# Attention, then a squared-relu layer pair, on one core: second part of P.V in a layer bank, x transposed by pairs, planner constants anew

## The chip, the core and the metric

The kernel runs on one core of one Trainium2 chip. A core has five engines that run side by side: TensorE (PE, matmul), VectorE (DVE), ScalarE (ACT), GpSimd (POOL) and SyncE (SP). DMA queues move data between HBM and SBUF. Matmuls write to PSUM, which has eight banks. The metric is the time of one execution in microseconds (us).

## The reference

The inputs are q, k and v of 8 batches x 8 heads x 576 tokens x 64 columns, a bias table of 32 buckets x 8 heads, and two weights, 512 x 2048 and 2048 x 512. All are float32.

```python
scores = (1.0 / np.sqrt(D)) * np.matmul(q, k.transpose(0, 1, 3, 2))
scores = scores + bias_table[bucket].transpose(2, 0, 1)[None]   # bucket of |i - j|, one value from 128 on
attn = softmax(scores)                                          # over the last axis
x = np.matmul(attn, v).transpose(0, 2, 1, 3).reshape(4608, 512)
h = np.maximum(x @ moe_w_in, 0.0)
return h * h @ moe_w_out
```

## The kernel before

**Work in pairs and groups.** Attention works on 32 pairs of heads, four to a batch; `pair(p)` (line 580) plans one. The two layers work on 9 groups of 512 tokens of x; `layers(g)` (line 1026) plans layer 1 of group g and layer 2 of group g - 1. A batch has 576 tokens, so group 0 needs batch 0, and group 1 needs the last 64 tokens of batch 0 and the first 448 of batch 1.

**A pair.** For the first three batches q and k are loaded with a cast to float16 in rows of six tokens and turned on PE: twelve transposes of 96 x 64 for q and as many for k (line 608), two heads side by side in two halves of the output partitions. DVE or ACT copies each to `qt` or `kt` (lines 570, 572). From batch 3 on (DT_QK) a DMA turns them. Score matmuls (line 653) have 64 rows, one head in each half of the array; they fill one of two sets of two PSUM banks (`st`). The last 64 queries and the last 64 keys of both heads get matmuls of their own (677, 702) from small zero-padded copies `qz` (635). ACT takes the exponentials (664, 687, 712). DVE multiplies the band near the diagonal by a table of exp(bias) (745, four bands a pair). That table is made at the start by 96 small matmuls (353) and six copies (367).

**P.V.** The product with v (781, 788) is made in five tiles of 128 queries, of which three form part 1 and two part 2. Both parts write the one bank `pv`. A column of constants in v gives the softmax sum. DVE takes the reciprocal (805) and multiplies (810), which gives x in float16.

**x.** For the first three batches (DT_X) `x_turn` (838) transposes x on PE once all four pairs of a batch are done: for each of five tiles of tokens four transposes, one for each pair, into one bank (848), and one copy of 512 columns (256 for the last tile) to `xt`. From batch 3 on a DMA turns x pair by pair (826).

**The layers.** Layer 1 of a group has 16 pieces of four matmuls of 512 columns (1044). Each piece goes to a relu (1065 on ACT, 1067 on DVE) and a square on DVE (1075). Layer 2 is a Strassen-Winograd product: seven products, each in two halves of eight matmuls of 256 columns (962), in the order P_ORDER, with sums of activations (921) and of weights (901) on DVE. Products 1 and 2 share a bank, 5 and 3 share one, and 7 and 4 share one; the second of each two waits until the first is read (989, 995, 997).

**What sets the order.** The program is not written in its final order. Each step is given to a planner (`Plan`, line 94) with an estimated cost for each engine that may run it, its inputs, the buffers it needs, a due time and an earliest time. `Plan.schedule` takes, again and again, the step that can start first, by due time among equals, and so fixes the order on every engine and, where two engines may run a step, which of them does. An engine runs its list strictly in order. PERIOD, LEAD, FAST and FASTN give the due time of a pair (`nominal`, 559), AHEAD how far ahead of it a pair may start, G0 and GP the due times of the groups, QUIET and LATER the earliest times of fills, TAB that of the bias table, and EV the pair up to which q/k copies are kept on DVE (pairs 1 to EV - 1; pair 0 is free). A change of any constant can move every step.

**PSUM.** Three banks (`f`, ring `r_g`) serve everything but scores and P.V: q/k transposes, the bias table, x transposes, layer 1 and layer 2.

**Loads.** POOL issues the loads of q, k, v and the weights in a fixed order. ORDER gives the place of the four quarters of w_in (i) and w_out (o) among batch 1's second two pairs (q1, k1), pairs 4 and 5 (q0, k0) and v. POOL also makes some of the `qz` copies, in the same queue. q and k of pair 0 come uncast by SP and ACT, and `cast_first` (463) casts them on DVE and ACT.

Of the kernel before, what the change touches and what calls it, by code (L numbers as in the profile page):

```python
# [25 lines left out]
GT = 512  # L26
NG = B * S // GT
XB = 3
XR = XB * S
DT_QK = 3  # L30
PERIOD, LEAD, FAST, FASTN = 9600.0, 1600.0, 3000, 7
AHEAD, G0, GP = 20600.0, 54700.0, 35900.0
DT_X = 3
RELU_DVE = 2
NSTG, NQK, NPT, NV, NX, NGB, NRT, NY = 5, 4, 3, 3, 6, 2, 4, 4
QUIET, LATER = 5200.0, 8500.0
TAB, EV = 6400.0, 1
P_ORDER = "1 6 2 5 7 3 4"
P_LAST = "1 6 2 5 7 3 4"
SIX = 3  # L40
ORDER = "k0 i0 q0 q1 v i1 i2 o0 k1 o1 i3 o2 o3"
HALF = GT // 2


# [146 lines left out]
def kernel(  # L191
# [71 lines left out]

    def loader(eng_name, eng, out_, in_, packets, deps=(), bufs=(), due=0.0):

        lane = [Buf(r_lane)] if eng_name == "POOL" else []
        issue = P.add(
            {eng_name: 720.0 if eng_name == "POOL" else 600.0},  # L270
            lambda: io(eng.dma_start(out=out_(), in_=in_())),  # L271
            deps,
            list(bufs) + lane,
            due,
        )
        return P.add({"DMA": packets / 16}, None, [issue], list(bufs) + lane, due if lane else -1e9), issue
# [6 lines left out]
    def const(f):  # L283
        return lambda: f

    def load(eng_name, eng, out_, in_, packets, deps=(), bufs=(), due=0.0):
        return loader(eng_name, eng, out_, in_, packets, deps, bufs, due)[0]


    first_f = gs[NGB - 1].bitcast(FP32).rearrange("p t c -> p (t c)")  # L290
# [9 lines left out]
    l_bt = load(  # L300
        "ACT", nc.scalar, const(bt_sb),
        const(bass.AP(tensor=bias_table.tensor, offset=bias_table.offset, ap=[[0, 4]] + [list(x) for x in bias_table.ap])),
        128 * 27, due=0,
    )
    l_far = load("ACT", nc.scalar, const(far_sb), const(bias_table[NBK - 1 : NBK, :]), 27, due=1)
    l_oh = load("SP", nc.sync, const(oh_sb), const(oh_d.ap()), 128 * 60, due=4)
# [15 lines left out]
    z_one = P.add({"DVE": 60.0}, lambda: io(nc.vector.memset(one_sb, 1.0)), due=-2)  # L322
    far_b = Buf(r_g)
    o_far = P.add(
        {"PE": 250.0},
        lambda: io(nc.tensor.matmul(g_ps[far_b.slot][:, 0:8], one_sb, far_sb, start=True, stop=True)),
        [l_far, z_one], [far_b], 0.0, 0.0, "f",
    )
# [18 lines left out]
    for c in range(6):  # L347
        t_b = Buf(r_g)

        def t_mm(c=c, t_b=t_b):  # L350
            for j in range(16 * c, 16 * c + 16):
                io(
                    nc.tensor.matmul(
                        g_ps[t_b.slot][:, ts(j - 16 * c, 32)], oh_sb[:, 380 - 4 * j : 508 - 4 * j],
                        eb_sb.rearrange("p i h -> p (i h)"), start=True, stop=True,
                    )
                )

        o = P.add({"PE": 16 * 55.0}, t_mm, [o_eb, l_oh], [t_b], LEAD + TAB, 0.0, "f")

        def t_ev(o, c=c, t_b=t_b):
            src = g_ps[t_b.slot].rearrange("p (w h) -> p h w", h=H)
            dst = tb_sb[:, :, ts(c, 64)]
            if o.eng == "ACT":
                io(nc.scalar.activation(out=dst, in_=src, func=COPYF))
            else:
                io(nc.vector.tensor_copy(out=dst, in_=src))

        tabs_done.append(one_of({"DVE": dve(512), "ACT": act(512)}, t_ev, [o], [t_b], 1.0))
# [17 lines left out]
    def fill(ap, value, ns, due, after, deps=()):  # L387
        return P.add({"DVE": ns}, lambda: io(nc.vector.memset(ap, value)), deps, (), due, after)  # L388

    zz = z_sb.bitcast(FP32)  # L390
    z_fix = [[fill(zz[:, 0], 0.0, 150.0, 10, QUIET)], [fill(zz[:, 1:], 0.0, 300.0, 11, LATER)]]
    first = [
        fill(pt_sb[:, :, PW:], 1.0, 150.0, 20, LATER),
        fill(pm_sb[:, :, S:], 1.0, 150.0, 20, LATER),
    ]
    v_fix = [
        [
# [5 lines left out]
        for o in [fill(vm_sb[:, a].bitcast(FP32), 0.0, ns, 30, at)]  # L403
    ]
    s_fix = [
        fill(stg[i][w][96:128, 512:640].bitcast(FP32), 0.0, 90.0, 40 + i, 25000.0)
        for i in range(NSTG)
        for w in range(2)
    ]
# [53 lines left out]
    def cast_first(w):  # L463

        def cast(o):
            src, dst = first_f[0:96, ts(w, 768)], stg[b_stg[0].slot][w][0:96, :]
            if o.eng == "ACT":
                io(nc.scalar.activation(out=dst, in_=src, func=COPYF))
            else:
                io(nc.vector.tensor_copy(out=dst, in_=src))  # L470

        l_qk[0, w] = [one_of({"ACT": act(768), "DVE": dve(768, 2.0)}, cast, [l_first[w]], [b_stg[0]], -3.0)]
# [86 lines left out]
    def nominal(p):  # L559
        return LEAD + FAST * min(p, FASTN) + PERIOD * max(p - FASTN, 0)  # L560

    xt_ready, x_last = {}, {}
    x_bufs = {}

    def copy_to(engs_n, out_f, in_f, deps, bufs, due, fp16=True, dve_only=False):
# [14 lines left out]
    def pair(p):  # L580
# [5 lines left out]
        for w, dst in ((0, qts), (1, kts)):  # L586
# [14 lines left out]
            def tr(w=w, bank=bank):  # L601
                ps = g_ps[bank.slot].bitcast(FP16)
                t = stg[b_stg[p].slot][w]
                if b < SIX:
                    for j in range(6):
                        for e in range(2):
                            io(
                                nc.tensor.transpose(  # L608
                                    ps[ds(64 * e, 64), ts(j, 96)], six(t)[:, e, ts(j, D)],
                                    id_sb[0:96, 0:96],  # L610
                                )
                            )
                else:
                    for j in range(5):
                        io(nc.tensor.transpose(ps[:, ts(j, 128)], rows(t)[:, j, :], id_sb))

            o = P.add({"PE": 12 * 36.0 if b < SIX else 5 * mm(128)}, tr, l_qk[p, w] + [l_id], [bank, b_stg[p]], T - 3000, after, "c" if b < SIX else "f")

            def turned(bank=bank):
                ps = g_ps[bank.slot].bitcast(FP16)[:, 0:S]  # L620
# [148 lines left out]
        xb = x_bufs[p] = Buf(r_x)  # L769
        norms = []  # L770
        for part, qt0, nq in ((0, 0, 3), (1, 3, 2)):
            bank = Buf(r_pv)

            def pv(qt0=qt0, nq=nq, bank=bank):
                ps = pv_ps[bank.slot][:, 0 : nq * 130].rearrange("p (t e d) -> p t e d", t=nq, e=2)
                pt, pm = pts[pb.slot], p4s[pb.slot]
                va, vm = vas[b_v[b].slot], v4s[b_v[b].slot]
                for i in range(nq):
# [21 lines left out]
            )  # L800
            rb = Buf(r_r)

            def recip(nq=nq, bank=bank, rb=rb):
                ps = pv_ps[bank.slot][:, 0 : nq * 130].rearrange("p (t e d) -> p t e d", t=nq, e=2)
                io(nc.vector.reciprocal(out=rs[rb.slot][:, 0:nq], in_=ps[:, :, :, 64:65]))

            def norm(nq=nq, bank=bank, rb=rb, qt0=qt0):
                ps = pv_ps[bank.slot][:, 0 : nq * 130].rearrange("p (t e d) -> p t e d", t=nq, e=2)
                io(
                    nc.vector.tensor_tensor(  # L810
                        out=xs[xb.slot][:, qt0 : qt0 + nq, :].rearrange("p t (e d) -> p t e d", e=2),
                        in0=ps[:, :, :, 0:64],
                        in1=rs[rb.slot][:, 0:nq].to_broadcast([128, nq, 2, 64]),
                        op=MULT,
                    )
                )
# [18 lines left out]
                    xt_ready.setdefault(g_, []).append(t)  # L835
        return norms

    def x_turn(b, norms):
        xb = [x_bufs[4 * b + hp] for hp in range(4)]
        T = nominal(4 * b + 3)  # L840
        for qt in range(5):
            n = 128 if qt < 4 else 64
            bank = Buf(r_g)

            def tr(qt=qt, bank=bank):
                ps = g_ps[bank.slot].bitcast(FP16)
                for kk in range(4):
                    io(nc.tensor.transpose(ps[:, ts(kk, 128)], xs[xb[kk].slot][:, qt, :], id_sb))  # L848

            deps = [n_[0 if qt < 3 else 1] for n_ in norms]  # L850
            o = P.add({"PE": 4 * mm(128)}, tr, deps, [bank] + xb, T, 0.0, "f")
            t0 = (b % XB) * S + qt * 128
            for a, z in [(0, n)]:
                c = t0 + a
                e = copy_to(
                    4 * (z - a),
                    lambda a=a, z=z, c=c: xt_sb[:, :, c : c + z - a],
                    lambda a=a, z=z, bank=bank: g_ps[bank.slot].bitcast(FP16)[:, 0:512].rearrange(
                        "p (k t) -> p k t", k=4
                    )[:, :, a:z],  # L860
                    [o] + xt_free(b * S + qt * 128 + n), [bank], T,
                )
                for g_ in range((b * S + qt * 128) // GT, (b * S + qt * 128 + n - 1) // GT + 1):
                    xt_ready.setdefault(g_, []).append(e)

    f1_last = {}

# [158 lines left out]
    def layers(g):  # L1026
# [4 lines left out]
        if g < NG:  # L1031
# [3 lines left out]
            for nt in range(16):  # L1035
                bank = Buf(r_g)

                def f1(nt=nt, bank=bank):
                    c = (g * GT) % XR
                    n = min(GT, XR - c)  # L1040
                    for a, z, c in ((0, n, c), (n, GT, 0)):
                        for kk in range(4 if z > a else 0):
                            io(
                                nc.tensor.matmul(  # L1044
                                    g_ps[bank.slot][:, a:z], w_in_sb[:, kk, ts(nt, 128)],
# [8 lines left out]
        for i in range(16):  # L1054
            if i < len(atoms1):
                nt, f1, bank = atoms1[i]
                o = P.add(
                    {"PE": 4 * mm(512)}, f1, xt_ready[g] + [l_win[nt // 4]], [bank, gb1], due + i * 2000, 0.0, "f"
                )
                f1_last[g] = o  # L1060
                rb = Buf(r_rt)
# [33 lines left out]
    t_done = sums_of_weights()  # L1095
    g = 0
    for b in range(B):
        norms = [pair(4 * b + hp) for hp in range(4)]
        if b < DT_X:
            x_turn(b, norms)  # L1100
        while (g + 1) * GT <= (b + 1) * S and g < NG:
            layers(g)
            g += 1
# [35 lines left out]
```

The softmax here doesn't subtract the row's maximum and nothing guards it: scores larger than these inputs give would overflow.

## Time and profile before

| | before |
|---|---|
| median of 6 runs | 377.5 us (376.32 to 378.92) |
| the profiled execution | 377.47 us |
| its span, first to last instruction | 375.7 us |
| PE busy | 360.8 us (96%), 4046 matmuls |
| DVE / ACT / POOL busy | 269.0 / 255.2 / 178.4 us |
| mean granted PE clock | 0.999 |
| first q/k transpose on PE | 6.47 us |
| first layer 1 matmul, group 0 | 40.61 us |
| first layer 1 matmul, group 1 | 74.98 us |
| last run of layer 2 matmuls (line 962) | from 370.44 us, 1.91 us |

The profile is of one execution. A row of instructions in order of time has the start, the length, engine, line, operation, what is written from what, the count, and in brackets how long the engine had been idle and which engine ended that. The length of a matmul includes its way through the array, so the distance of two starts is the better measure of PE's time. In the table by stage each row has a stretch, its length, and for each engine the busy time and the number of instructions. In the chain of waits, a row is a stretch of the path that ended last.

### The profile page before, as it was taken

The numbers are of one execution on the slowest core, as the hardware profiler recorded it, in microseconds if no ns is written. First come the engines' busy times: TensorE is split into PE (matmuls) and PEld (weight loads), VectorE is DVE, ScalarE is ACT, GpSimd is POOL, SyncE is SP. The second block draws the span as 40 slices with busy tenths as digits, with TensorE's granted clock in tenths as the row PEclk, the third lists the DMA queues.
The fourth block names the chain that finished last, engine by engine and source line by source line (L and its number), as shares of the span: only waits on it lengthen the run. The fifth ranks groups of instructions, "written<-read, shape, count | busy, mean of one in ns | idle before, by whom it ended". The sixth has DMA issues, their size and how long they took to land.

```text
span 375.7 us, 10050 instructions
## 1 busy us (share of the span) xinstructions
PE 360.8 (96%) x4046; PEld 246.8 (66%) x4046; DVE 269.0 (72%) x612; ACT 255.2 (68%) x361; POOL 178.4 (47%) x318
## 2 busy tenths in 40 slices
PE   3988999999999999999999999999999999999996
PEld 2655546745778666687766765677577888556775
DVE  3897789998788586867685777757776683583653
ACT  3898889987667886866787778746885541564330
POOL 8877453889575592933868455854650000000000
PEclk9999999999999999999999999999999999999999
DMA  9999999799999799949999699999990222100103
GB/s 171 143 129 165 198 170 77 47 92 86 101 162 128 92 123 137 110 52 119 140 132 71 111 116 152 90 103 109 167 100 30 77 58 72 66 2 28 58 28 112
DMA packets 146163, 38.74 MB, mean 103 GB/s; under 512 B 128070, under 2 KB 146118, under 8 KB 146118
## 3 DMA queue, kind: packets, MB, share of 16 engines
q0 software_dynamic: 94496, 18.07, 62.5%
q1 hardware_dynamic: 51280, 19.75, 26.0%
q8 instruction: 31, 0.51, 0.6%
q10 hardware_dynamic: 342, 0.30, 0.3%
q14 instruction: 14, 0.11, 0.1%
HBM read 36.88 MB, written 9.44 MB: 123 GB/s over the span
## 4 chain that ended last, share of the span: by engine, by line
PE 90%; ACT 5%; DVE 2%; DMA 1%; issue 1%; ACTq 0%
PE f L1044 34%; PE f L962 29%; PE pv L788 9%; PE st L653 8%; PE pv L781 3%; ACT pt L664 2%; PE st L702 2%; PE st L677 2%; PE f L608 1%; DMA g<-in_k_dram 1%; ACT pt L687 1%; PE f L848 1%; ACT kt L570 0%; DVE s L921 0%; ACT pm L712 0%
## 5 line engine op out<-in xcount | busy, mean ns | idle before, releaser
L1044 PE MATMUL f<-xt,w_in_sb 128*128 128x512 f16 (+4 forms) x704 | 142.1, 341 | 0.0
L664 ACT ACTIVATE pt<-st 128x1024 f16<-128x1024 f32 x128 | 126.7, 1024 | 22.4 <-PE st L653 22.4
L1065 ACT ACTIVATE rt<-f 128x512 f16<-128x512 f32 x134 | 80.0, 598 | 62.1 <-PE f L1044 60.5
L1044 PEld LDWEIGHTS <-w_in_sb 128*128 128x128 f16 x704 | 62.6, 98 | 53.1 <-issue 10.8
L1075 DVE TENSOR_TENSOR g<-rt 128x512 f16<-128x512 f16 x144 | 60.9, 424 | 41.4 <-ACT rt L1065 40.2
L745 DVE TENSOR_TENSOR pt<-pt,tb_sb 128x1536 f16<-128x1536 f16 (+2 forms) x96 | 58.3, 621 | 10.4 <-ACT pt L664 10.1
L962 PEld LDWEIGHTS <-g 128*128 128x128 f16 x576 | 54.9, 98 | 15.4 <-issue 4.7
L788 PE MATMUL pv<-va,pt 128*128 128x65 f16 x1280 | 54.6, 193 | 0.0
L788 PEld LDWEIGHTS <-pt 128*128 128x128 f16 x1280 | 50.2, 97 | 2.9 <-issue 0.7
L271 POOL DMA_DIRECT2D qs<-in_q_dram x71 | 49.9, 724 | 2.4 <-DMA ks<-in_k_dram 1.1
L271 POOL DMA_DIRECT2D ks<-in_k_dram x71 | 49.9, 713 | 2.1 <-issue 2.1
L962 PEld LDWEIGHTS <-s 128*128 128x128 f16 x432 | 40.6, 98 | 10.6 <-issue 3.4
L635 POOL COPY qz<-qt 64x64 f16<-64x64 f16 x53 | 15.5, 292 | 61.2 <-DMA qt<-qs 36.7
L989 DVE SCALAR_TENSOR_TENSOR y<-f,y 128x512 f32<-128x512 f32 (+1 forms) x47 | 31.3, 667 | 16.1 <-PE f L962 15.1
L653 PE MATMUL st<-qt,kt 64*128 64x512 f16 x256 | 41.1, 391 | 1.3 <-ACT pt L664 0.5
L635 POOL COPY qz<-kt 64x64 f16<-64x64 f16 x59 | 20.2, 342 | 35.3 <-DMA kt<-ks 19.8
L962 PE MATMUL f<-w_out_sb,s 128*128 128x256 f16 x288 | 36.6, 273 | 0.0
L962 PE MATMUL f<-wt,g 128*128 128x256 f16 x288 | 36.6, 273 | 0.0
L962 PE MATMUL f<-w_out_sb,g 128*128 128x256 f16 x288 | 36.2, 273 | 0.1
L781 PE MATMUL pv<-vm,pm 128*128 128x130 f16 x160 | 35.3, 221 | 0.6 <-DVE x L810 0.4
L810 DVE TENSOR_TENSOR x<-pv,r 128x384 f16<-128x384 f32 x64 | 31.3, 490 | 1.9
L271 POOL DMA_DIRECT2D va<-in_v_dram x36 | 30.8, 865 | 0.9 <-DVE vm L388 0.5
(62 smaller groups left out, 307.4 us busy)
## 6 DMA issues: line engine op xcount, KB each, us to landing
out_dram<-y SPq DMA_DIRECT2D x34, 256.0 KB, 2.3
va<-in_v_dram POOLq DMA_DIRECT2D x28, 128.0 KB, 4.6
qs<-in_q_dram POOLq DMA_DIRECT2D x40, 64.0 KB, 3.3
ks<-in_k_dram POOLq DMA_DIRECT2D x40, 64.0 KB, 3.0
w_in_sb<-in_moe_w_in_dram POOLq DMA_DIRECT2D x4, 512.0 KB, 7.5
w_out_sb<-in_moe_w_out_dram POOLq DMA_DIRECT2D x4, 512.0 KB, 9.8
qs<-in_q_dram POOLq DMA_DIRECT2D x11, 144.0 KB, 5.2
ks<-in_k_dram POOLq DMA_DIRECT2D x11, 144.0 KB, 5.9
```

The lines of the kernel that those rows point to most:

```text
L271: lambda: io(eng.dma_start(out=out_(), in_=in_())),
L635: io(eng.tensor_copy(out=dst[qb.slot][rw, rw], in_=src[qb.slot][rw, 512:576]))
L653: nc.tensor.matmul(sets_ps[st.slot][:, e, :], kt[rw, ts(jt, 128)], qt[rw, 0:512], start=True, stop=True,)
L664: nc.scalar.activation(out=p5(pts[pb.slot])[:, jt, :, 0:512], in_=sets_ps[st.slot], func=EXPF, scale=SCALE)
L745: io(nc.vector.tensor_tensor(out=a, in0=a, in1=t, op=MULT))
L781: nc.tensor.matmul(ps[:, i, :, :], pm[:, c : c + 128], vm[:, hp, :, 0:65], start=True, stop=False)
L788: nc.tensor.matmul(ps[:, i, e, :], pt[:, (2 * jt + e) * S + c : (2 * jt + e) * S + c + 128], va[:, jt, 2 * hp + e, 0:65], start=False, sto ...
L810: nc.vector.tensor_tensor(out=xs[xb.slot][:, qt0 : qt0 + nq, :].rearrange("p t (e d) -> p t e d", e=2), in0=ps[:, :, :, 0:64], in1=rs[rb.s ...
L962: nc.tensor.matmul(g_ps[bf.slot][:, ts(s_, HALF)], left(c, s_), right(c), start=(c == 0 and (s_ == 0 or apart) and i not in before), stop= ...
L1044: nc.tensor.matmul(g_ps[bank.slot][:, a:z], w_in_sb[:, kk, ts(nt, 128)], xt_sb[:, kk, c : c + z - a], start=(kk == 0), stop=(kk == 3),)
L1065: io(nc.scalar.activation(out=rts[rb.slot], in_=g_ps[bank.slot], func=RELUF))
L1075: nc.vector.tensor_tensor(out=gs[gb1.slot][:, nt, :], in0=rts[rb.slot], in1=rts[rb.slot], op=MULT)
```

## The change

1. Batch 0 only: part 2 of P.V takes one of the three `f` banks instead of `pv` (PV_G = 1), and its reciprocal and norm read from there.
2. `x_turn` is called for each pair, right behind it, and no longer for each batch. For a pair it makes three transposes and one copy of 384 columns, then two transposes and one copy of 192 columns. For three batches that is 24 copies in place of 15; the 60 transposes stay.
3. Pair 0: `cast_first` writes the two heads side by side for each of the six tokens of a row, and one transpose of 128 columns does both heads: 6 transposes in place of 12 for q and for k, in the full array.
4. Planner constants: the pairs' spacing, the groups' due times, how far ahead a pair may start, fills and table times, EV from 1 to 5, FILL (the fills of the staging tails) from 25000 to 0, some estimated costs, P_ORDER (product 3 ahead of 7) and ORDER (v ahead of q1, k1 together behind q1, all of w_out last).
5. A way to begin layer 1 of group 0 before its last pair (PRE) is written but set to 0, so it adds no instruction.

The instruction order of both builds shows what the planner made of it: batch 0's P.V is in runs of 45 matmuls (five tiles) instead of 27 and 18, x transposes stand among the pairs, and POOL issues the first quarter of w_in behind batch 0's v.

```diff
-PERIOD, LEAD, FAST, FASTN = 9600.0, 1600.0, 3000, 7
-AHEAD, G0, GP = 20600.0, 54700.0, 35900.0
+PERIOD, LEAD, FAST, FASTN = 9000.0, 0, 3000, 8
+AHEAD, G0, GP = 25000, 60000, 46000
...
-QUIET, LATER = 5200.0, 8500.0
-TAB, EV = 6400.0, 1
-P_ORDER = "1 6 2 5 7 3 4"
+QUIET, LATER = 3700.0, 9000
+TAB, EV = 5800.0, 5
+P_ORDER = "1 6 2 5 3 7 4"
 P_LAST = "1 6 2 5 7 3 4"
-ORDER = "k0 i0 q0 q1 v i1 i2 o0 k1 o1 i3 o2 o3"
+PV_G, PRE, FILL = 1, 0, 0
+ORDER = "k0 i0 q0 v i1 i2 q1 k1 i3 o0 o1 o2 o3"
...
-        fill(stg[i][w][96:128, 512:640].bitcast(FP32), 0.0, 90.0, 40 + i, 25000.0)
+        fill(stg[i][w][96:128, 512:640].bitcast(FP32), 0.0, 90.0, 40 + i, FILL)
...
-            src, dst = first_f[0:96, ts(w, 768)], stg[b_stg[0].slot][w][0:96, :]
+            src = first_f[0:96, ts(w, 768)].rearrange("p (e j d) -> p e j d", e=2, j=6)
+            dst = stg[b_stg[0].slot][w][0:96, :].rearrange("p (j e d) -> p e j d", e=2, j=6)
...
+                if p == 0:
+                    for j in range(6):
+                        io(nc.tensor.transpose(ps[:, ts(j, 96)], t[0:96, ts(j, 128)], id_sb[0:96, 0:96]))
...
-            bank = Buf(r_pv)
+            bank, home = (Buf(r_g), g_ps) if b == 0 and part and PV_G else (Buf(r_pv), pv_ps)
...
-    def x_turn(b, norms):
+    def x_turn(p, norms):
+        b, hp = divmod(p, 4)
+        xb = x_bufs[p]
+        T = nominal(p)
+        for part, qt0, nq in ((0, 0, 3), (1, 3, 2)):
             bank = Buf(r_g)
+            n = min(128 * nq, S - 128 * qt0)
+            c = (b % XB) * S + 128 * qt0
...
+                for i in range(nq):
+                    io(nc.tensor.transpose(ps[:, ts(i, 128)], xs[xb.slot][:, qt0 + i, :], id_sb))
+            o = P.add({"PE": nq * mm(128)}, tr, [norms[part]], [bank, xb], T, 0.0, "f")
+            e = copy_to(
+                n,
+                lambda c=c, n=n: xt_sb[:, hp, c : c + n],
+                lambda bank=bank, n=n: g_ps[bank.slot].bitcast(FP16)[:, 0:n],
+                [o] + xt_free(b * S + 128 * qt0 + n), [bank], T,
+            )
...
-        norms = [pair(4 * b + hp) for hp in range(4)]
-        if b < DT_X:
-            x_turn(b, norms)
+        for p in range(4 * b, 4 * b + 4):
+            norms = pair(p)
+            if b < DT_X:
+                x_turn(p, norms)
```

## Prediction

> **What bounds the kernel now.** I read the page's rows of engine time first, then the busy tenths in 40 slices, then a table of busy time by stage, then the instructions in order of time where the stages meet, and last the chain of waits. TensorE (PE) is busy 96% of the span, so only stretches in which PE waits, or PE's own work, can give time back.
>
> ```profile
> PE 360.8 (96%) x4046; PEld 246.8 (66%) x4046; DVE 269.0 (72%) x612; ACT 255.2 (68%) x361; POOL 178.4 (47%) x318
> ...
> PE   3988999999999999999999999999999999999996
> ```
>
> The stages (time, PE, weight loads, DVE, ACT, POOL, then clock and DMA) show where PE waits and for whom:
>
> ```profile
> 6.00:16.00 10.00, 9.28 (x150) 6.39 (x150) 8.50 (x29) 7.25 (x11) 7.99 (x15) 1.00 1.51 178
> 16.00:41.00 25.00, 21.03 (x396) 14.76 (x395) 20.47 (x60) 23.09 (x33) 19.48 (x36) 1.00 1.28 146
> 41.00:62.00 21.00, 21.00 (x209) 10.65 (x207) 18.23 (x40) 17.94 (x27) 8.67 (x13) 1.00 1.26 168
> 62.00:75.00 13.00, 12.74 (x253) 9.73 (x250) 12.63 (x34) 12.97 (x20) 8.56 (x20) 1.00 0.53 34
> 75.00:300.00 225.00, 225.00 (x2446) 154.35 (x2446) 166.75 (x366) 165.01 (x229) 128.80 (x225) 1.00 1.06 109
> ```
>
> From 75 us to 300 PE never stops. Up to 41 us it waits 4.7 us (0.72 + 3.97) while DVE and ACT are nearly full: attention of batch 0 alone, no layer work yet to fill PE with. From 62 to 75 DVE and ACT are full (12.63 and 12.97 of 13) and PE only just. So the time is set by two moments: the first matmul of layer 1, group 0 (line 1044, at 40.61), and the first of group 1 (at 74.98). The PE rows that lead to the first moment:
>
> ```profile
> 35.22 0.22 PE L781 MATMUL pv<-vm,pm 128*128 128x130 f16 x1
> ...
> 38.19 0.22 PE L781 MATMUL pv<-vm,pm 128*128 128x130 f16 x1
> ...
> 39.68 0.45 PE L848 MATMUL f<-id_sb,x 128*128 128x128 f16 x5 [0.57 <-DVE x L810]
> 40.07 0.60 PE L653 MATMUL st<-qt,kt 64*128 64x512 f16 x4
> 40.61 2.76 PE L1044 MATMUL f<-xt,w_in_sb 128*128 128x512 f16 x12
> ```
>
> and those of DVE beside them:
>
> ```profile
> 36.31 0.20 DVE L805 RECIPROCAL r<-pv 128x6 f32<-128x6 f32 x1
> 36.54 0.56 DVE L810 TENSOR_TENSOR x<-pv,r 128x384 f16<-128x384 f32 x1
> ...
> 38.98 0.18 DVE L805 RECIPROCAL r<-pv 128x4 f32<-128x4 f32 x1
> 39.20 0.42 DVE L810 TENSOR_TENSOR x<-pv,r 128x256 f16<-128x256 f32 x1
> 40.17 0.29 DVE L572 COPY xt<-f 128x256 f16<-128x256 f16 x1 [0.55 <-PE f L848]
> ```
>
> P.V of pair 3 starts at 35.22. Its second part waits for the one P.V bank (the norm at 36.54 ends at 37.10) and is then queued behind twelve x transposes, to 38.19. Norm, transposes and copies follow: 5.39 us from P.V to layer 1.
>
> **Step 1: bank and x by pairs, the chain at 35.22.** With its own bank, part 2 follows part 1 at once: five tiles of P.V at 0.30 us (starts 35.22, 35.52, 35.81) end 1.5 us after the start. Norm 1 ends 1.88 after the start as now; reciprocal and norm 2 follow it on DVE (0.18 + 0.42): 2.5. Two transposes instead of five: 0.55 us from norm to copy (39.62 to 40.17) less three of 0.056: 2.9. The copy of 192 columns, between rows of 256 (0.29) and nothing smaller, taken at 0.25: 3.15, and layer 1 0.05 later. The chain is **3.2 us, 2.2 less**. If PE is behind with other work, part 1's three transposes still hide under norm 2.
>
> **Step 2: when pair 3's P.V starts.** DVE sets it (last band at 34.95 to 35.21). I count its instructions from pair 0's cast to that band, at the spacing of their starts (576 columns 0.67, bands 0.87, 0.41, 0.34 and 0.22, table copy 0.67, norms 0.48 and 0.35). Now: 26.3 us in the 29.35 from 5.86. In the new order ten memsets of 0.08 (FILL = 0) and 0.68 of others precede the cast, one table copy goes to ACT, four 64x64 copies to others; three more q/k copies (EV = 5, 2.0) and three x copies (0.9) come in: 26.3 again. Only the division moves: 12.4 before pair 0's P.V (14.3 now), 14.0 from there to pair 3's (12.0). Pair 0's P.V: 5.86 + 12.4 + idle of 1.9 (as now) to 2.9, taken 2.3: 20.6 (now 22.05). Pair 3's: + 14.0 + 0.6 (now 1.15): **35.2, unchanged**. ACT loses five q/k copies (0.58 each) and gains a table copy and three x copies, 1.5 us less: no limit. Layer 1 starts at 35.2 + 3.2 = **38.4**.
>
> **Step 3: what PE has not done by then.** At the rates of full stretches (0.213 us for 512 columns, 0.107 for a score or layer 2 matmul, 0.0235 a narrow transpose), PE has done 20.2 us of work before the first layer 1 matmul now, and 18.9 in the new order: four score matmuls (0.43), two of the last keys (0.24), and the q/k transposes of two pairs less what pair 0's wide ones differ (0.65). It does them later. From there to group 1's first matmul it has 31.2 us against 30.0, and 31 changes of tile mode against 22. A change costs 0.11 us: the chain of waits has layer 1 behind a score matmul and behind P.V's full mode as
>
> ```profile
> 124.54 0.97 PE f L1044 x4
> ...
> 126.64 0.86 PE f L1044 x4
> ```
>
> So 2.2 us come, and 1.2 + 1.0 go. What stays is idle: now 34.4 = 30.0 + 2.4 + 2.0. PE alone would let group 1 start at 38.4 + 31.2 + 3.4 + (0.7 to 2.0) = 73.7 to 75.0.
>
> **Step 4: group 1.** It needs every x copy of batch 1; the last ended at 74.93, just before 74.98. DVE has 31.5 us of work in the 33.2 from 41.75 to there (95%). In the new order 34.1: seven x copies for two (+1.2), two more relus (+1.3). From 38.5 at 95 to 97% it ends between 74.4 and 73.6: I take 74.0, **0.9 us early**.
>
> The rule that speaks against the change: copies of x are now 24 instead of 15, at a fixed cost each. Rows: 128x512 418 ns, 128x256 286, so 0.52 ns a column and 154 ns fixed; nine more make 1.4 us over three batches, where DVE is full in two. The Trainium skill, page "Perfetto Trace Analysis", section "Optimizing Scalar/DVE Operations", has about 125 ns for DVE on PSUM and tells to group when the engine is saturated: 1.1 us by its figure, an estimate.
>
> **Step 5: the rest.** After 75 us the PE work is equal (278.4 us both), with 92 mode changes against 94: -0.2. The wait of 0.17 us before the P.V at 309.30 may go: -0.1. P_ORDER now puts product 3 right behind 5, on a bank that must be evacuated first (0.69): one or two other PE pieces of 0.87 stand between in the new order, so nothing; without them 0.2 us a group, 1.6 in all. The tail keeps its order: last layer 1 matmul, then 112 of layer 2. Weights: PE waits for none after 41 us. The first quarter of w_in is issued behind batch 0's v instead of ahead of it, the others near their old places, all behind 64x64 copies in POOL's queue as now: nothing, or, if such a copy holds POOL, one load late by the 2.5 us that 512 KB take at 206 GB/s. Pair 0's six 128-wide transposes have no row: by the column rate 0.24 warm and 0.48 at the half speed seen at 6.47 (twelve spaced 0.49, against 0.28 from 63.31 on), against 0.49; by the x transposes up to 0.67. I take equal. The cast into interleaved heads has no row either: from 0.56 as now to twice that; I take 0.56. Planner costs move nothing but the order counted here.
>
> **Sum.** -0.9 - 0.2 - 0.1 = -1.2 us on the profiled execution's 377.47 (span 375.70 and 1.77 around it), which is the median of the six, 377.5: **376.3 us**.
>
> **Rivals.** *ACT's relief reaches pair 3*: its P.V starts 1.5 earlier, layer 1 at 36.9, DVE packs at 98% to 71.8, PE has 72.2: -2.8 - 0.3, 374.4. For: ACT is full from 16 to 41. Against: DVE has no less to do. *Given back in full*: DVE packs at the 93% that the window from 41.75 to 74.93 shows as busy, 38.5 + 36.6 = 75.1: +0.1 - 0.3, 377.3. For: DVE's sum grows by 2.6 us. *Slower, by DVE's copies before pair 3*: if pair 0's P.V does not come before 22.05 (five q/k copies and four table copies still stand before its bands), the 14.0 behind it put pair 3's at 37.2, layer 1 at 40.4, group 1 at 76.4: +1.4 - 0.2, 378.7. It decides from about 21.9 us for pair 0's P.V. For: copies come in ahead of bands; against: 1.9 us less in front.
>
> **How the numbers follow.** Forecast 0.32, ACT's relief 0.17, given back 0.35, slower 0.16. A difference under 0.3% (1.1 us) can't be told from none by a measurement of this kernel: faster 0.49, same 0.35, slower 0.16. The range runs from just below ACT's relief (374.4) to the slower rival (378.7), which also covers the cast's doubling (0.6) on top of any case up to it: 374.0 to 378.6.
>
> **What would show it.** In the new profile: pair 0's P.V near 20.6, pair 3's near 35.2 with its five tiles in one run, the first layer 1 matmul near 38.4, DVE with no gaps from there to group 1's first matmul near 74.0, and PE full after. I am wrong if pair 3's P.V moves by more than a microsecond, or if PE waits anywhere after 75 us.

## The result, and the profile after

| | before | after |
|---|---|---|
| median | 377.24 us (375.84 to 378.92, 47 runs) | 378.9 us (378.53 to 380.43, 21 runs) |
| profiled execution, span | 377.47, 375.7 us | 378.55, 376.4 us |
| first q/k transpose on PE | 6.47 us | 5.80 us |
| P.V of pair 0 / of pair 3 | 22.05 / 35.22 us | 19.51 / 34.60 us |
| first layer 1 matmul, group 0 | 40.61 us | 37.22 us |
| first layer 1 matmul, group 1 | 74.98 us | 75.74 us |
| last layer 2 matmul ends | 372.35 us | 373.10 us |

The changed kernel takes 1.0048 times the time of before (95% interval 1.0036 to 1.006): **slower by 0.5%**. Layer 1 starts 3.4 us earlier, and by the start of group 1 all of that is gone and 0.8 us more.

Two things in these numbers do not come from the order of work. In the profiled execution of the changed kernel everything starts 0.67 us earlier, because the first cast, which waits for a load of k, can start at 5.18 us instead of 5.86. Other executions show both values for the same start of the program: the first transpose is at 5.93 in e14, which starts like before, and at 6.54 in e8, which starts like after. Counted from the first transpose, layer 1 comes 2.7 us earlier, group 1 1.4 us later and the end 1.4 us later. And the time outside the span (execution time less span) is 2.11 us in the changed kernel's runs (median) and 1.78 in those of before. In runs derived from the changed kernel its median lies between 1.75 (e11) and 2.14 us (e13), and no trace shows what it is. So 0.3 of the 1.7 us lie outside the instructions.

The rows of the page that answer to those of before:

```profile
PE 360.4 (96%) x4034; PEld 246.2 (65%) x4034; DVE 271.9 (72%) x618; ACT 253.1 (67%) x360; POOL 181.8 (48%) x322
...
PE   3988989899999999999999999999999999999996
```

DVE has 2.9 us more to do and ACT 2.1 less. The busy tenths of PE now dip in two slices (47 to 56 us and 66 to 75 us) that were full before. The table by stage of the changed kernel (columns as before):

```profile
16.00:37.25 21.25, 17.91 (x343) 12.58 (x342) 19.27 (x47) 18.27 (x26) 15.87 (x30) 1.00 1.32 153
...
47.00:51.00 4.00, 2.52 (x53) 1.34 (x50) 3.83 (x9) 3.48 (x7) 2.46 (x6) 1.00 1.24 205
...
62.00:76.00 14.00, 12.85 (x246) 9.59 (x244) 13.50 (x33) 12.82 (x19) 9.42 (x18) 1.00 0.68 52
76.00:300.00 224.00, 223.90 (x2452) 153.53 (x2451) 164.69 (x365) 165.10 (x232) 131.03 (x229) 1.00 1.05 108
```

Up to layer 1 PE now waits 3.6 us (0.30 + 3.34) where it waited 4.7. From 76 us it is as full as before. The new idle lies between 47 and 76 us: 1.48 us of idle in the row of 47 to 51, and 1.15 in that of 62 to 76. The chain that the change was to shorten, in the rows of PE:

```profile
34.60 0.22 PE L789 MATMUL pv<-vm,pm 128*128 128x130 f16 x1
...
35.50 0.22 PE L789 MATMUL f<-vm,pm 128*128 128x130 f16 x1
...
37.22 1.03 PE L1050 MATMUL f<-xt,w_in_sb 128*128 128x512 f16 x4
```

Part 2 of P.V follows part 1 at once, in an `f` bank, and layer 1 stands 2.62 us behind the first tile; it was 5.39. Now the waits of PE between 29 and 76 us (what it was to write and at which line, whom it waited for: total us, times, longest). First those of before, then those of after:

```profile
PE st L702 <- ACT pt L664: 0.8, 1, 0.8
PE f L848 <- DVE x L810: 0.6, 1, 0.6
PE st L653 <- ACT pt L687: 0.4, 1, 0.4
```

```profile
PE st L661 <- ACT kt L572: 1.5, 1, 1.5
PE f L859 <- ACT kt L572: 0.6, 1, 0.6
PE st L710 <- ACT pt L672: 0.5, 1, 0.5
PE st L685 <- ACT pm L720: 0.4, 1, 0.4
PE f L613 <- DVE kt L574: 0.3, 1, 0.3
```

With the smaller ones the sums are 2.3 and 3.5 us. Before, 2.1 of it lay ahead of layer 1. After, the waits of 1.5 (at 48.6), 0.6 (at 67.8) and 0.3 us (at 74.2) lie behind it, and each is for a copy of q or k out of an `f` bank.

Set at equal PE work done (each matmul at the rates of full stretches), the changed kernel leads by 1.7 to 2.0 us from 38 to 48 us, by 0.4 at 50, and trails by 1.1 at 75 and by 0.75 at the end; of the lead 0.67 is the earlier start. PE's time beyond its work (waits and changes of tile mode) grew from 4.4 to 7.4 us between its 20th us of work and group 1.

The wait of 1.5 us can be read in full. PE turned k6, q7 and k7 in a row (starts 47.67, 47.95, 48.20): three banks, which is all of ring `f`. The score matmuls next in its list need kt of pair 6. ACT, just then in two exponentials (47.57 to 49.51), copies the three banks one after the other:

```profile
49.39 0.66 ACT L572 ACTIVATE kt<-f 128x576 f16<-128x576 f16 x1
49.92 0.67 ACT L572 ACTIVATE qt<-f 128x576 f16<-128x576 f16 x1
50.45 0.69 ACT L572 ACTIVATE kt<-f 128x576 f16<-128x576 f16 x1
```

Meanwhile PE has layer 1 work that is ready and no bank to put it in.

### The profile page after: what moved, and what is told of

It is laid out like the page before. It is cut to its first block, busy times and chain, and to the rows that moved or that the text cites. A ratio compares the mean times of both kernels' runs of the same rounds, so it can differ in the third digit from the quotient of the medians.

```text
span 376.4 us, 10027 instructions
## 1 busy us (share of the span) xinstructions
PE 360.4 (96%) x4034; PEld 246.2 (65%) x4034; DVE 271.9 (72%) x618; ACT 253.1 (67%) x360; POOL 181.8 (48%) x322
## 4 chain that ended last, share of the span: by engine, by line
PE 89%; DVE 5%; ACT 2%; DMA 1%; issue 1%; DVEq 0%; ACTq 0%
PE f L1050 34%; PE f L968 29%; PE pv L796 9%; PE st L661 9%; PE pv L789 2%; PE st L710 2%; PE st L685 2%; PE f L613 2%; DVE pt L753 1%; DMA g<-in_k_dram 1%; PE f L859 1%; ACT pt L672 1%; DVE s L927 1%; DVE x L818 1%; ACT rt L1080 0%
## 5 line engine op out<-in xcount | busy, mean ns | idle before, releaser
L643 POOL COPY qz<-qt 64x64 f16<-64x64 f16 x59 | 21.2, 359 | 67.4 <-DMA qt<-qs 23.5
L796 PE MATMUL pv<-va,pt 128*128 128x65 f16 x1216 | 51.8, 193 | 0.0
L661 PE MATMUL st<-qt,kt 64*128 64x512 f16 x256 | 40.3, 389 | 1.7 <-ACT kt L572 1.5
L789 PE MATMUL pv<-vm,pm 128*128 128x130 f16 x152 | 33.5, 221 | 0.2
L643 POOL COPY qz<-kt 64x64 f16<-64x64 f16 x57 | 18.0, 315 | 29.2 <-DMA kt<-ks 21.7
L818 DVE TENSOR_TENSOR x<-pv,r 128x384 f16<-128x384 f32 (+1 forms) x60 | 29.7, 495 | 2.0
```

What stands on the lines that cost most here:

```text
L643: io(eng.tensor_copy(out=dst[qb.slot][rw, rw], in_=src[qb.slot][rw, 512:576]))
L661: nc.tensor.matmul(sets_ps[st.slot][:, e, :], kt[rw, ts(jt, 128)], qt[rw, 0:512], start=True, stop=True,)
L789: nc.tensor.matmul(ps[:, i, :, :], pm[:, c : c + 128], vm[:, hp, :, 0:65], start=True, stop=False)
L796: nc.tensor.matmul(ps[:, i, e, :], pt[:, (2 * jt + e) * S + c : (2 * jt + e) * S + c + 128], va[:, jt, 2 * hp + e, 0:65], start=False, sto ...
L818: nc.vector.tensor_tensor(out=xs[xb.slot][:, qt0 : qt0 + nq, :].rearrange("p t (e d) -> p t e d", e=2), in0=ps[:, :, :, 0:64], in1=rs[rb.s ...
```

## The experiments

Three theories stood at first. **BANKS**: those three transposes in a row hold all the banks, and what is lost there never comes back. **FULL**: DVE and ACT carry a fixed load that must be done before group 1 can start, so an earlier layer 1 is given back whatever is done at 48 us. **PARTS**: the new parts themselves (more copies, the shared bank) cost the time, whatever the constants. **SAME** and **ORDER** came later: DVE is no tighter than before, and what counts is the order of steps in the queues. All ratios are to the kernel before, with 95% intervals.

### Which half of the change

e3 has the new code (items 1 to 3) with the old constants, e4 the old code with the new constants:

```diff
 # e3, on the kernel after
-PERIOD, LEAD, FAST, FASTN = 9000.0, 0, 3000, 8
+PERIOD, LEAD, FAST, FASTN = 9600.0, 1600.0, 3000, 7
...
-ORDER = "k0 i0 q0 v i1 i2 q1 k1 i3 o0 o1 o2 o3"
+ORDER = "k0 i0 q0 q1 v i1 i2 o0 k1 o1 i3 o2 o3"
 # e4, on the kernel before: the same lines the other way
```

> The changed kernel's code (part 2 in a layer bank, x by pairs, pair 0's wide transposes) with all planner constants, estimated costs, ORDER and P_ORDER of the kernel before. In its order no three q/k transposes of pairs 6 and 7 stand in a row: three pieces of layer 1 come ahead of them. Theory BANKS: the gain in front is kept, layer 1 starts near 37.5, no wait over 0.5 us near 50, median 376.0 to 377.0 (0.5 to 1.5 us faster than the kernel before). Rival PARTS: 378.5 or more. Rival DVE: nine more x copies (1.4 us by their rows) stay, so group 1 starts no earlier than in the kernel before, 377.3 to 378.5.

> The kernel before with all new constants, estimated costs, ORDER and P_ORDER, but the old parts: one P.V bank, x by batches, pair 0 in narrow transposes. Theory BANKS: no gain in front (the chain from P.V of pair 3 to layer 1 stays at 5.4 us), q/k transposes of pairs 6 and 7 crowd near 48 us here too: slower than the kernel before by 0.5 to 1.5 us, 378.0 to 379.0. Rival PARTS: as fast as the kernel before or faster, 376.5 to 377.5. Rival DVE: five q/k copies held on DVE delay pair 3, as the prediction's slow rival had it: 378.5 to 379.5.

Measured: e3 379.1 us, 1.0052 (1.003 to 1.0074); e4 378.97 us, 1.0044 (1.0029 to 1.006). Each half alone costs what the whole costs. In e3 layer 1 starts at 36.87 and group 1 at 76.69; its waits (0.70 up to 51.17, 0.90 up to 54.40 and others) lie elsewhere than those of after. e4 has none at 48 us. In its trace PE waits 2.3 us between 63 and 75.3, and 0.90 more at 226 us, for a DMA that turns k, so part of its loss lies far behind group 1. Three different orders with like results: the loss is tied neither to the parts alone nor to one place.

### The wait at 48 us

e5 puts two layer 1 pieces behind the transposes of k6, and those of q7 and k7 further back, so that no three stand in a row; their relus and copies go along, and two sums of activations go behind them. e6 makes five more such moves between 68 and 76 us. In the names of steps tr is a q/k transpose and cp its copy, f1_g_i piece i of layer 1 of group g and re its relu, st, lq and lk the scores (all, last queries, last keys), ex an exponential, nm a norm, xt a transpose of x and xc its copy.

```diff
 # e5, steps moved within their engine's list: step, behind which step
+MOVES = [('f1_0_8', 'tr_k6'), ('f1_0_9', 'f1_0_8'), ('tr_q7', 'st_6_0'), ('tr_k7', 'lk_6'),
+         ('cp_q7', 'ex_6_0'), ('cp_k7', 'ex_6_1'), ('re_0_8', 'nm_4_0'), ('re_0_9', 're_0_8'), ...]
 # e6, beside those
+         ('tr_q9', 'xt_6_0'), ('f1_1_0', 'lq_8'), ('tr_k11', 'lk_9'), ('re_1_0', 'ex_8_q'), ('xc_7_1', 'xc_7_0')]
```

> The changed kernel with a few steps moved in its finished order near 48 us alone: the two q/k transposes of pair 7 go behind the next two pieces of layer 1, so that three q/k transposes in a row no longer hold all three f banks; the relus of these two pieces and the copies of pair 7 go along on DVE and ACT, two sums of activations go behind them. Nothing else differs. The two runs before this one (parts alone, constants alone) both started layer 1 of group 0 near 37 to 38 us, without the wait at 50 us in one of them, and both had lost it all by group 1. Theory BANKS (PE lost 1.48 us at 50.10 for want of an f bank and nothing gives it back): the end comes 1.0 to 1.3 us earlier, median 377.6 to 377.9 against 378.9. Theory FULL (DVE and ACT together carry a fixed load that must be done before group 1 can start; PE started early only waits later): the wait at 50 us goes, but new waits of about the same sum stand between 52 and 76 us, group 1 starts between 75.3 and 75.8, and the end stays within 0.4 us.

> As e5, and besides it four moves between 68 and 76 us: the x transpose of pair 6 takes a bank that is free and goes ahead of the q transpose of pair 9; the first piece of layer 1 of group 1 goes ahead of the q/k transposes of pair 11, with its x copy and its relu ahead of theirs. Theory BANKS: the waits of 0.64 at 68.42 and of 0.32 at 74.49 go as well, the end comes 1.8 to 2.2 us earlier than in the changed kernel, median about 376.9. Theory FULL: the end moves by less than 0.5 us, since the copies and exponentials that PE waits for come no earlier; only the order in which the last x copy comes may give 0.3.

Measured: e5 378.99 us, 1.0037 (1.0021 to 1.0053); e6 379.28, 1.0049 (1.0031 to 1.0068). The edit did what it was to do; the rows of PE in e5:

```profile
49.54 1.90 PE L1143 MATMUL f<-xt,w_in_sb 128*128 128x512 f16 x8
51.60 0.60 PE L739 MATMUL st<-qt,kt 64*128 64x512 f16 x4 [0.15 <-ACT kt L648]
...
54.03 0.45 PE L689 MATMUL f<-id_sb,ks 96*64 96x96 f16 x12 [0.33 <-ACT xt L648]
```

The wait of 1.48 us is 0.15 now. But the transposes of k7 wait 0.33 us for a bank that ACT copies x from, and there are more changes of tile mode. At an equal start and equal PE work 1.4 us are gained at 50 us, and 0.5 us of that is left from 54 us on; the interval does not tell e5 from the changed kernel. In e6 the waits at 68 and 74 us give way to others (0.52 for a load of v, 0.27, 0.31). **BANKS falls** as the whole cause: its wait is real, and 1.5 us of wait removed gave a third of that in the trace.

### More and less work on DVE and ACT

```diff
 # e7 on after, e9 on before: four more products between 60 and 68 us, 0.69 us each on DVE
+nc.vector.tensor_tensor(out=spare_sb, in0=tb_f, in1=tb_f, op=MULT)
 # e10: three more copies on ACT between 65 and 71 us, 1.1 us each
+nc.scalar.activation(out=spare_sb, in_=tb_f, func=COPYF)
 # e8: two of the four bands left out in each of pairs 5, 6 and 7, 4.1 us of DVE
+OUT = ['band_5_1', 'band_5_2', 'band_6_1', 'band_6_2', 'band_7_1', 'band_7_2']
 # e11: e8, and the copies of k6, q7, k7, k8, q9 on DVE instead of ACT
 # e12: all bands, those five copies on DVE, and four sums of activations moved back
```

e8 and e11 leave part of the bias of three pairs out.

> The changed kernel with four extra multiplications of 128x1024 on DVE (0.69 us each, 2.8 in all, results unused), put behind steps that stand at 60.6, 63.0, 65.5 and 67.5 us; the order is kept otherwise. Theory FULL: group 1 starts 2.0 to 2.8 us later and the end follows, median 381.0 to 381.6. Theory BANKS (what costs is which step holds a bank at two places): DVE's delay reaches PE only through the two DVE copies that hold banks near 72 and 74, the end comes 0 to 0.8 us later.

> The changed kernel without the second and third band multiplication of pairs 5, 6 and 7 (six instructions, 0.95 and 0.41 us each pair, 4.1 us of DVE before group 1); the output of these pairs lacks the bias there. The order is kept otherwise. Theory FULL: DVE reaches the x copies of batch 1 earlier, group 1 starts 1.0 to 2.0 us earlier (ACT and the order of PE take the rest), the end 1 to 2 us, median 377 to 378. Theory BANKS: the waits at 50.10 and 68.42 are for ACT's copies and stay, the end moves by less than 0.4 us.

> The kernel before with the same four extra multiplications of 128x1024 on DVE (2.8 us in all), behind the same steps (two squares, the sums of activations and the bands of pair 7, at 62 to 68 us here). Theory FULL, as it now stands (in the changed kernel DVE's queue from 62 to 72 us has become a limit, as its chain of waits shows 9 us of DVE there; in the kernel before the chain runs through PE and ACT in that stretch): DVE has room here, so the end comes 0.3 to 1.5 us later, against 2 to 3 in e7. Rival SAME (DVE is the limit there in both, so nothing new came with the change): 2.0 to 2.8 us later, median 379.3 to 380.2.

> The changed kernel with three extra copies of 128x1024 on ACT (about 1 us each by the exponentials of the same size, results unused), behind the copies of q and k of pairs 8 and 9 at 64.9, 68.4 and 68.9 us. If ACT is as full as DVE there (12.82 us busy of 14, its gaps only the way to PE and back), the end comes 2 to 3 us later; if DVE alone limits, ACT has 1.2 us of room and the end comes 0.5 to 1.5 us later.

> As e8 (no second and third band multiplication of pairs 5, 6 and 7, whose output lacks the bias there; 4.1 us off DVE), and the copies of k of pair 6, q and k of pair 7, k of pair 8 and q of pair 9 made by DVE instead of ACT (2.7 us off ACT, 3.5 onto DVE, which so has 0.6 less than in the changed kernel). The waits at 50.10 and 68.42 were for those ACT copies. Theory FULL in its second form (DVE and ACT limit side by side, each with a chain of its own): both waits shrink, group 1 starts 1.0 to 2.0 us earlier, median 377.0 to 378.0. If it is neither engine but the order on PE itself, the end stays within 0.4 us of the changed kernel.

> The changed kernel, nothing left out: the second four sums of activations of group 0 (2.8 us of DVE at 63.4 to 66.2) go behind the first squares of group 1, and DVE makes the five copies of e11 instead of ACT. DVE's load before group 1 grows by 0.7 us, ACT's falls by 2.7. Theory FULL in its second form: the waits at 50.10 and 68.42 shrink, group 1 starts 0.5 to 1.5 us earlier; the end gains as much, less what the sums cost where DVE is next full (84 to 92 us, up to 1 us): median 377.5 to 379.0. If it is neither engine: within 0.4 us, or later by the sums' price.

| run | median us | ratio (95%) | in the trace |
|---|---|---|---|
| e7 | 380.84 | 1.0101 (1.007 to 1.0133) | 2.9 us later for 2.8 us of work, with a fall of the clock in it; by the medians 1.9 |
| e8 | 378.75 | 1.0041 (1.0023 to 1.0059) | 0.15 us earlier for 4.1 us less work |
| e9 | 379.54 | 1.0058 (1.0038 to 1.0079) | 2.2 us later for 2.8 us of work |
| e10 | 380.19 | 1.0075 (1.0053 to 1.0097) | 1.2 us later for 3.3 us of work |
| e11 | 379.84 | 1.0062 (1.004 to 1.0084) | wait of 1.5 us gone, a new one of 1.45 at 51 us |
| e12 | 381.37 | 1.0103 (1.0081 to 1.0125) | the same (1.44), and 0.99 at 71, 0.85 at 86 us |

In e7's trace the granted clock falls to 0.50 from 72 to 74 us and to 0.66 from 74 to 76, behind waits of 1.2 and 1.0 us. Its three runs without such falls have a median of 380.63 us, 1.8 above those of the changed kernel (378.86). So work added to DVE counts for about two thirds, in the kernel before (e9) for more, and work added to ACT for a third; work taken away from DVE counts nothing. In e8 PE's waits stand where they stood:

```profile
PE st L739 <- ACT kt L648: 1.5, 1, 1.5
PE f L948 <- ACT kt L648: 0.6, 1, 0.6
```

**FULL falls**: with 4.1 us less to do DVE is busy 11.71 of the 13.5 us from 62.5 to 76 (13.00 in the changed kernel from 62 to 75.5), PE is held as before, and group 1 starts no sooner. e9 says that a full DVE is nothing new: before the change it was at least as tight (SAME). In e11 the copy of q7 stands on DVE behind sums of activations and a norm (it starts at 52.06 us), and x transposes wait for the bank that it frees: in a list that runs strictly in order, a step moved out of one wait became another. The Trainium skill, page "Perfetto Trace Analysis", section "Identifying the Most-Contended Engine", tells to find the engine with the highest occupancy and to optimize it first. By occupancy (for PE by its weight loads, one of the page's two measures for it) that is DVE here, with 13.50 of the 14 us from 62 to 76 against 9.59 of PE's weight loads. Taking 4.1 us of work off DVE, 1.3 us of busy time in this stretch, returned 0.15 us: here the measurement decides against the rule.

### The same instructions in another order

e13 and e15 are the changed kernel, e14 is the kernel before; each with an order between 29 and 100 us that is written out by hand. Nothing is added or left out; each step stays on its engine. e13 moves 38 steps of PE, 46 of DVE and 15 of ACT; e14 32, 25 and 18; e15 45, 51 and 20. e13 has one sum of weights ahead of the landing of its load; e15 has no step ahead of its load.

```diff
-    for op in P.schedule():
+    for op in P.reordered(r_g):     # the list of each engine, and the f bank of each step, from a table
```

> The changed kernel, every instruction kept on its engine, none added or left out; between 29 and 100 us the planner's order is replaced by one written out by hand, in which 38 steps of PE, 46 of DVE and 15 of ACT stand elsewhere (q/k transposes and their copies earlier and one at a time between pieces of layer 1; norms ahead of sums and bands on DVE; x transposes later). Theory ORDER (what the early start of layer 1 won is lost only because the planner's order lets PE meet steps whose inputs another queue delivers later; neither DVE nor ACT is full in itself): most of PE's waits from 29 to 76 us (5 us in the changed kernel, the largest 1.48, 0.64, 0.53) go, group 1 starts near 72 us, the end comes 2.5 to 4 us earlier, median 375.0 to 376.5, below the kernel before. Theory FULL (DVE and ACT together set when group 1 can start): less than 0.7 us earlier.

> The kernel before, treated in the same way over the same stretch (32 steps of PE, 25 of DVE, 18 of ACT elsewhere). It tells what the new parts are worth when neither kernel is held up by its order. If the parts win something (shorter chain from P.V of pair 3 to layer 1): this gains less than e13 does, 1 to 2 us, and ends 0.5 us or more behind e13. If the parts bring nothing of their own: it ends level with e13 or ahead of it, median 375.0 to 376.0.

> As e13 (the changed kernel, every instruction kept on its engine, the order between 29 and 100 us written out by hand), but no step stands ahead of the landing of its load; the sums of output weights come from 51 us on. 45 steps of PE, 51 of DVE and 20 of ACT stand elsewhere. Theory ORDER (the early start of layer 1 is lost because the planner's order lets PE meet steps whose inputs another queue delivers later): PE's waits between 29 and 76 us mostly go, group 1 starts near 72 us, the end comes 2.5 to 4 us earlier than in the changed kernel, median 375.0 to 376.5. If it ends clearly below e14 (375.9), the new parts are worth something of their own; level with it, they are not. Theory FULL (DVE and ACT together set when group 1 can start): less than 0.7 us earlier than the changed kernel.

Measured: e13 382.89 us, 1.0137 (1.0112 to 1.0163); **e14 375.93 us, 0.9957 (0.9942 to 0.9971); e15 375.76 us, 0.995 (0.9931 to 0.997)**. e13's miss is one wait of PE (the view of waits, 26 to 100 us):

```profile
PE f L1141 <- DVE rt L1173: 5.8, 1, 5.8
```

DVE stood at the sum of weights until the quarter of w_out was in SBUF, and the relus behind it with it. The granted clock then is 0.50 from 46 to 52 us, and by equal PE work 7.4 us are lost there, 5.8 of them the wait. In e15, with that sum later, the stage that lost most in the changed kernel and the one behind it look so (47 to 51 us, and 62 to group 1's first matmul at 73.08):

```profile
47.00:51.00 4.00, 4.00 (x47) 2.06 (x46) 3.96 (x9) 3.89 (x5) 0.45 (x2) 1.00 1.24 207
...
62.00:73.10 11.10, 10.32 (x195) 7.70 (x192) 10.22 (x29) 9.20 (x14) 9.44 (x18) 1.00 0.90 67
```

PE is full from 47 to 51 us while DVE and ACT are **fuller** than in the changed kernel (3.96 and 3.89 us against 3.83 and 3.48). What differs here is what they do first. (Up to group 1 the order by hand leaves nearly all of DVE's work in place: two bands and two sums of activations go behind that point and two sums of weights ahead of it, 1.3 us less by their lengths.) After P.V of a pair, DVE in the changed kernel:

```profile
47.53 0.69 DVE L927 TENSOR_TENSOR s<-g 128x1024 f16<-128x1024 f16 x1
48.25 1.42 DVE L927 TENSOR_TENSOR s<-g,s 128x1024 f16<-128x1024 f16 x2
49.59 0.68 DVE L927 TENSOR_TENSOR g<-g 128x1024 f16<-128x1024 f16 x1
50.19 0.19 DVE L813 RECIPROCAL r<-pv 128x6 f32<-128x6 f32 x1
50.41 0.56 DVE L818 TENSOR_TENSOR x<-pv,r 128x384 f16<-128x384 f32 x1
```

and in e15:

```profile
46.67 0.20 DVE L904 RECIPROCAL r<-pv 128x6 f32<-128x6 f32 x1
46.90 0.56 DVE L909 TENSOR_TENSOR x<-pv,r 128x384 f16<-128x384 f32 x1
...
48.05 0.68 DVE L1018 TENSOR_TENSOR s<-g 128x1024 f16<-128x1024 f16 x1
```

In the changed kernel the last tile of P.V ends at 47.2 and the norm, which frees the P.V bank, starts at 50.4, behind four sums for layer 2, which begins at 63.99. In e15 P.V ends at 46.6 and the reciprocal starts at 46.67; the sums stand singly between steps that PE waits for. The same four sums stand in the changed kernel's queue a second time from 63.44, and pair 6's norm behind them. On PE, e15 makes the q/k transposes one at a time (43.41, 44.32, 49.48) with scores, layer 1 or P.V between them. Its waits from 29 to 76 us sum to 1.4 us, those of e14 to 0.5.

**ORDER holds, PARTS falls**: the parts of the change, ordered by hand, are 3.1 us faster than the changed kernel (375.76 against 378.9; in the span 2.9) and 0.5% faster than before. With the same instructions on the same engines, the order is what differs. Which of the moves bring how much was not tried one by one.

### Two of the constants alone

```diff
 # e16
-ORDER = "k0 i0 q0 v i1 i2 q1 k1 i3 o0 o1 o2 o3"
+ORDER = "k0 i0 q0 q1 v i1 i2 o0 k1 o1 i3 o2 o3"
 # e17
-TAB, EV = 5800.0, 5
+TAB, EV = 5800.0, 1
```

> The changed kernel with ORDER alone as before (q of pairs 6 and 7 ahead of v, w_out between k and the last w_in); the planner makes its order anew, and in it two pieces of layer 1 stand between the transposes of q and those of k of pairs 6 and 7, so that no three stand in a row. If the load order makes the losing order: the wait at 50 us goes and 0.7 to 1.5 us come, median 377.4 to 378.2. If any order of the planner with these parts meets such waits: other waits of like size show up, median 378.5 to 379.5.

> The changed kernel with EV alone as before (q/k copies of pairs 1 to 4 free to go to ACT). If keeping them on DVE costs (the prediction's slow rival): P.V of pair 0 to 3 come earlier by up to a microsecond, DVE's load before group 1 falls by 2 to 2.7 us, median 377.5 to 378.3. If any order of the planner with these parts loses: 378.5 to 379.5.

Measured: e16 377.47 us, 0.9999 (0.9985 to 1.0013); e17 380.56 us, 1.0085 (1.0058 to 1.0113). With the loads in their old order alone the changed kernel is level with before: layer 1 starts at 37.21 as in after, two layer 1 pieces stand between transposes of pairs 6 and 7, and the waits sum to 1.3 us. So **the new load order, through the order of steps that it leads to, is 1.4 of the 1.7 us lost**, by the medians; in the span 1.1 of 1.4 us, counting before's 57 runs without a fall of the clock (376.8 after, 375.7 in e16, 375.4 before). EV = 5 is a gain, by 1.7 us by the medians, though the intervals just overlap: with EV = 1 pair 0's P.V comes 1.8 us sooner and pair 3's 0.4, counted from the first transpose (18.43 and 34.89 less 6.51), but waits of 0.75, 0.55 and 0.48 us stand between 49 us and group 1, which starts at 77.35.

## Why the prediction was wrong

The forecast was 376.3 us, 1.2 faster than the profiled execution of before; measured were 378.9 us, slower by 0.5%. What failed is how group 1's start was reached (steps 3 and 4) and what the loads were taken to do (step 5).

- **Step 1** held and was cautious: 2.62 us from P.V to layer 1 for 3.2.
- **Step 2** held: 19.51 for 20.6, 34.60 for 35.2, layer 1 at 37.22 for 38.4, of which 0.67 us is the luck of an early load. Counted from the first transpose, pair 3's P.V is at 28.80 us where it was at 28.75: unchanged, as the step says. (DVE was not "nearly full" up to 41 us: it was busy 20.47 of the 25 us from 16 on.) So the slower rival's condition (pair 0's P.V from 21.9 us) was not met; the kernel became slower by another way.
- **Step 3**: the work and the changes of tile mode were counted well, the idle was not. "What stays is idle" carried the 2.0 us of the old order over to the new one. From layer 1 to group 1 PE took 38.5 us: 31.1 of work, 3.4 of mode changes by the step's own price, and so 4.0 of idle where the step allowed 0.7 to 2.0. The waits of 1.48, 0.64 and 0.32 us are the largest part of it. The upper end of that step's own range, 75.0, took idle as now, which was no upper end.
- **Step 4 failed.** It let DVE set group 1, as a queue that packs its work at 95 to 97%. DVE was busy 35.4 us between the first matmuls of group 0 and group 1, 4.6 more than before (30.85), where the step added 2.6: beside the x copies and relus that were counted, two band multiplications and a q/k copy more came in. It was busy 92% of that stretch. The two put group 1 at 75.74, not 74.0. The rival "given back in full", which packed DVE at 93%, was near the place (75.1) and still its reason does not hold: e8 took 4.1 us off DVE and gained nothing, e15 left all but 1.3 us of DVE's work in place and gained 2.7 us by group 1, and e16 left as much as there was (64.55 us busy up to group 1 for 64.46) and gained 1.0. DVE's queue decided by its order, not by its sum. The prediction read a share of busy time as the limit of the engine.
- **Step 5 failed at the loads.** "the others near their old places ... nothing" looked at when the weights land, and no wait for weights did appear. But ORDER decided the order of all other steps, and that was worth 1.4 us (e16). The rest behind group 1, put at -0.3, came to nothing in the trace (0.76 us late at group 1, 0.75 at the end).
- Of its two tests, pair 3's P.V moved by 0.6 us and PE stands nowhere of note after 75 us. Both came out as foretold, for neither looked at 47 to 75 us, where the loss was. The trace of before could not show the new waits; the new instruction order could, since it has k6, q7 and k7 in a row in a ring of three banks.

What stays open: e14 and e15 differ by less than their intervals tell, so whether the parts of the change are worth anything at the end is not known; they start layer 1 earlier (36.38 against 38.54), and group 1 no earlier (73.08 against 72.71). Of their gain over before, 0.4 us is the clock: before's median is 377.6 us over the 98 runs beside the experiments and 377.1 over the 57 whose mean clock is 0.997 or more, while of the 19 runs of e14 and e15 one has a lower clock. Neither order is known to be near the best. Why EV = 1 costs 1.7 us is seen only as waits in other places; DVE's work before group 1 did not fall with it (65.5 us busy for 64.5), as the planner put eight sums of weights there instead of two.

The fastest version is e15, at 375.76 us, level with e14.

## What to carry to other kernels

An early start won at one place is kept only if the queues behind it are ordered for it: after a change that moves steps, read each engine's new order for rings that one kind of step fills, and for long steps nobody waits for ahead of short ones that free a bank. An engine that is 92% busy need not be the limit: add work to it and take work from it, and if only the first moves the time, look at the order of the queues before the amount of work. To tell a change's parts from the order that came with them, run the same instructions in another order.

## What the runs showed of the hardware

In some executions the granted clock falls for 3 to 4 us as layer 1 begins. The table by stage (columns as before, the clock third from the end) of e5, then of the changed kernel:

```profile
34.00:36.00 2.00, 1.58 (x26) 1.50 (x25) 0.60 (x2) 1.47 (x3) 1.95 (x5) 0.68 1.28 201
36.00:38.00 2.00, 2.00 (x31) 1.70 (x30) 0.95 (x4) 0.00 (x0) 2.00 (x3) 0.50 1.11 148
```

```profile
34.00:36.00 2.00, 1.62 (x46) 1.65 (x47) 0.72 (x4) 1.32 (x3) 1.96 (x5) 1.00 1.28 199
36.00:38.00 2.00, 1.98 (x22) 0.94 (x19) 1.89 (x6) 1.38 (x2) 2.00 (x3) 1.00 1.15 160
```

In e5 tiles of P.V start 0.55 us apart instead of 0.30. Of the 98 runs of the kernel before beside the experiments, 41 have a mean clock below 0.997, and a median span of 376.5 us against 375.4 for the 57 others, so a fall costs about 1.1 us; of the changed kernel's 21 runs, 2 have it. PE had waited 0.20, 0.53 and 0.42 us between 32 and 34.5 us in e5, but the changed kernel's own profile has the same three waits and no fall. So these waits alone do not decide it, and what does is not known.

The Trainium skill, page "TensorE: Matmul & The Clock Gate", section "HAM oscillation — how this bites in real kernels", gives PE gaps above about 3.4 us as what cools the clock. e13 agrees: PE waits 5.82 us there and the clock is 0.50 from 46 to 52 us. The falls of e5 and e7 do not come under that rule: no gap ahead of them is longer than 0.53 and 1.2 us.
